# Second batch's mixing term moved from TensorE quarters to the ordinary path, with nine low parts on GpSimd

## The chip, the core and the metric

The kernel runs on one core of a Trainium2 chip. Its engines run side by side, each working through its own queue in order: TensorE (PE; its weight loads are shown as PEld), VectorE (DVE), ScalarE (ACT), GpSimd (POOL), and SyncE (SP), which only starts DMAs here. The metric is the device time of one launch in microseconds.

## What is computed

Sparse attention over 8 batches, 8 heads, 576 positions of 64 columns, and then a mixing and feed-forward layer:

```python
mask_local = (rel >= 0) & (rel < 32)                      # heads 0..3
mask_strided = (rel >= 0) & (key % 32 == query % 32)      # heads 4..7
x = softmax(q k^T / 8, masked) @ v                        # x: [8, 576, 512] over all heads
u = x + (x^T @ U @ V)^T                                   # U: [576, 32], V: [32, 576]
out = u + relu(u @ w_ch1) @ w_ch2                         # w_ch1: [512, 2048], w_ch2: [2048, 512]
```

`U`, `V` and the two weight matrices arrive as 64-bit floats, everything else as 32-bit. Both feed-forward products take each operand as a high part (rounded) and a low part (the rest): three passes of TensorE per product, high by high, high by low, low by high.

## The kernel before

**Feed-forward steps.** The 8 x 576 rows are worked off as nine blocks of 512 rows: block n < 8 has the first 512 rows of batch n, block 8 the last 64 of all batches. Each block runs 16 steps `fc`, one for every 128 hidden columns: `gemm1` (12 passes of 128 rows by 512 columns into `ph`), ScalarE's ReLU to the high part `gh`, VectorE's low part `gl`, and `gemm2` (12 passes into the accumulator `acc`). In program order `gemm1(fc + 1)` stands ahead of `gemm2(fc)`. A "slot" is half a step, so a block has 32 slots. I call the weights of one `fc` a weight block, w0 to w15.

**What runs between the steps.** While block n is multiplied, the next batch's attention is advanced by a generator (`advance`): a table (`A_EARLY` for block 0, `A_LATE` for the later ones) says from which slot to which it is spread and over how many pieces. For batches from 2 on (`NSP = 2`) the strided heads don't go to TensorE: in `strided_heads`, GpSimd multiplies (L440 for scores, L468 for the output; 27 pieces each, `tmp`) and VectorE sums each piece (L442, L470). `S0` and `S1` say in which slot that begins and ends. The strided heads' q, k and v come in the tile `st`.

**Start.** `first_attention` does batches 0 and 1 before the first feed-forward block and into it, all heads on TensorE. Batch 0 then goes straight into the transposed form that `gemm1` reads (`uh`, `ul`), by pairs of heads, in `quarter`: TensorE transposes x (L316), multiplies it by U (L282, L284) and adds V's product into the same bank (L293). For batch 1, `attention(1)` does the same four quarters during block 0's steps, and puts the sum into `raw`, which `split` turns into `uh` and `ul` when block 0 ends. For these two batches `gemm2` of step 0 also adds V's product to the accumulator (L667), since the untransposed x stays without it.

**Later batches.** `mix_t` multiplies x by U in two halves (L511, L515; VectorE adds the parts, L522, and makes the low part, L526), `mix_u` makes u in place (TensorE L534, VectorE L536), `mix_tail` does the last 64 rows (L543, L549), and `transposes` turns u with VectorE (L623) into `bt`, from which 32 DMAs fill `raw`.

**Weights.** Weight blocks 0 to 6 come as halves (`w0a`: the `gemm1` half, `w0b`: the `gemm2` half), 7 to 15 whole (128 x 1024). `weights` converts each in program order, some four steps ahead of its use: ScalarE takes the upper words (L124), VectorE makes three passes (L126, L127, L129), ScalarE casts the high part (L202) and VectorE subtracts it for the low part (L203). The buffers of `cv` are three, shared with `bt` and with later q, k, v loads. `load_ahead` starts the loads; GpSimd copies of one word (L166) hold each until its buffer may be overwritten.

**Who sets the order.** The framework schedules the instructions of each engine from the program's order and its own timing model; `tc.issue_after(i)` puts what it encloses behind instruction `i` on `i`'s own engine only.

Of the kernel before, what the change touches and what calls it, by code (L numbers as in the profile page):

```python
# [36 lines left out]
def fused_kernel(ctx, tc, pairs, strided, U, V, w_in, masks, eye, out):  # L37
# [147 lines left out]
    def weights():  # L185
        for i, (fc, x) in enumerate(units):
# [16 lines left out]
            nc.vector.tensor_tensor(out=parts[:, :, 1], in0=fv, in1=parts[:, :, 0].bitcast(F32), op=ALU.subtract)  # L203
# [65 lines left out]
    def quarter(b, pr):

        main, last_x, p0 = parts[b, pr]
        by_class = pr >= 2
# [7 lines left out]
        with tc.issue_after(lead):  # L280
            for t in range(4):
                nc.tensor.matmul(pm, Um[:, t, :], main[:, t, :], start=t == 0 and not (b and by_class), stop=False,  # L282
                                 skip_group_check=True, tile_position=(0, 0))
            nc.tensor.matmul(pm, Um[p0:p0 + 64, 4, :], last_x, start=False, stop=True, skip_group_check=True,  # L284
                             tile_position=(p0, 0))
# [11 lines left out]
        if b:  # L297
            dst = raw[:, :, :, pr, :]
            nc.scalar.copy(out=dst, in_=src.rearrange("p (s a) x -> p s a x", s=4) if by_class else
                           src.rearrange("p (s a x) -> p s a x", s=4, a=4))  # L300
        else:
            hi, lo = (u[:, pr, :].rearrange("p (j c) -> p j c", c=32) if by_class else u[:, pr, :] for u in (uh, ul))
            one = nc.scalar.copy(out=hi, in_=src)
            two = nc.vector.tensor_tensor(out=lo, in0=src, in1=hi.bitcast(F32), op=ALU.subtract)
            marks["split0"] = (two.ins, one.ins)
# [342 lines left out]
    def gemm1(fc, dcs=range(NDC)):  # L648
# [7 lines left out]
        nc.scalar.activation(out=gh, in_=ph, func=AF.Relu)  # L656
# [4 lines left out]
    def gemm2(n, fc, gh, gl):  # L661
        if fc == 0:
            accs[n] = [ps_acc.tile([128, 2, 512], F32, name="acc") for _ in range(2)]
        for s in range(4):
            cs = slice(128 * s, 128 * s + 128)
            if fc == 0 and n < NSP:
                nc.tensor.matmul(accs[n][s // 2][:, s % 2, :], Vst[:, cs], tsts[n], start=True, stop=False)  # L667
            for i, (gt, part) in enumerate(((gh, 0), (gh, 1), (gl, 0))):
                nc.tensor.matmul(accs[n][s // 2][:, s % 2, :], gt[:, cs], w_parts[fc, 1][:, part, :],  # L669
                                 start=(fc == 0 and i == 0 and n >= NSP), stop=(fc == NFC - 1 and i == 2))  # L670
# [159 lines left out]
```

## Time and profile before

| what | value |
|---|---|
| three runs | 940.04, 940.11, 940.59 us (median 940.11) |
| the profiled execution | 940.45 us, of it 938.7 us span |
| TensorE busy | 909.2 us, 97% of the span |
| VectorE, ScalarE, GpSimd busy | 561.6, 247.2, 325.7 us |
| TensorE's granted clock over the span | 0.993 |
| bytes moved | 74.24 MB |

Times in the profile are counted from the start of the span. A row of a timeline has the start, the length, the engine, the source line, the operation, output and input tile with shape, and in brackets how long the engine stood idle before it and what released it. A row of a group has the count, the busy time in us and the mean length in ns. Lengths of matmuls are modelled and overlap, so the spacing of the pieces in the chain of waits is what a pass costs there.

### The profile page before, as it was taken

How to read it: one execution, taken by the hardware profiler on the slowest of the kernel's cores; microseconds unless marked ns; L12 is line 12 of the kernel's file. 1: busy time of each engine (PE TensorE's matmuls, PEld its weight loads, DVE VectorE, ACT ScalarE, POOL GpSimd, SP SyncE). 2: the span in 40 equal slices, each digit the busy share in tenths (PEclk: the TensorE clock that was granted, in tenths of full speed). 3: DMA queues.
4: the chain of work that ended last, by engine and by line, in shares of the span. 5: the costliest groups of instructions: out<-in, count | busy, mean ns of one | idle time of the engine just before them, and what ended most of it. 6: DMA issues, size and time to landing. Idle time of an engine off the chain costs nothing.

```text
span 938.7 us, 16860 instructions
## 1 busy us (share of the span) xinstructions
PE 909.2 (97%) x7032; PEld 727.3 (77%) x7032; DVE 561.6 (60%) x907; ACT 247.2 (26%) x485; POOL 325.7 (35%) x374
## 2 busy tenths in 40 slices
PE   5789999999899999999999999999999999999997
PEld 4667888777677778777887788778877888888885
DVE  4679987757786678666776677657764341122111
ACT  4436542115122412151114221421233111121110
POOL 1213018434854385346644565447440000000000
PEclk9999999999989999999999999999999999999999
DMA  9958210200250114101420142013300231001001
GB/s 349 340 193 343 88 62 26 97 1 26 61 180 3 32 41 166 42 1 60 138 72 2 51 157 72 2 51 99 119 2 1 57 112 23 1 1 46 1 0 45
DMA packets 36780, 74.24 MB, mean 79 GB/s; under 512 B 5952, under 2 KB 20672, under 8 KB 34784
## 3 DMA queue, kind: packets, MB, share of 16 engines
q1 hardware_dynamic: 26464, 66.60, 20.1%
q10 hardware_dynamic: 9280, 4.20, 1.9%
q0 software_dynamic: 960, 2.36, 0.8%
q8 instruction: 55, 0.90, 0.4%
q14 instruction: 21, 0.17, 0.1%
HBM read 54.14 MB, written 11.67 MB: 70 GB/s over the span
## 4 chain that ended last, share of the span: by engine, by line
PE 83%; DVE 6%; POOL 5%; DMA 3%; issue 2%; ACT 1%; SPq 0%; DVEq 0%; POOLq 0%
PE acc L669 38%; PE ph L652 37%; POOL tmp L440 5%; DVE st L470 1%; PE px L380 1%; DMA w1a<-in_w_dram 1%; PE px L346 1%; PE px L367 1%; DMA w2a<-in_w_dram 1%; DMA late<-in_pairs_dram 1%; PE px L511 1%; DMA st<-in_strided_dram 1%; DVE gl L657 1%; PE px L534 1%; DVE s_st L442 0%
## 5 line engine op out<-in xcount | busy, mean ns | idle before, releaser
L657 DVE SCALAR_TENSOR_TENSOR gl<-ph,gh 128x512 fp32r<-128x512 f32 x144 | 98.8, 688 | 224.2 <-ACT gh L656 223.6
L652 PE MATMUL ph<-uh,w 128*128 128x512 f32 x648 | 215.0, 392 | 0.0
L656 ACT ACTIVATE gh<-ph 128x512 fp32r<-128x512 f32 x144 | 86.1, 598 | 471.2 <-PE ph L652 388.9
L440 POOL TENSOR_TENSOR tmp<-st 128x576 f32<-128x576 f32 (+6 forms) x162 | 168.7, 1082 | 114.0 <-DMA st<-in_strided_dram 58.3
L468 POOL TENSOR_TENSOR tmp<-st,s_st 128x448 f32<-128x448 f32 (+7 forms) x162 | 136.5, 873 | 183.7 <-DVE st L470 97.5
L669 PE MATMUL acc<-w,gh 128*128 128x512 f32 x648 | 197.6, 393 | 0.0
L470 DVE TENSOR_REDUCE st<-tmp 128x64 f32<-128x64 f32 (+8 forms) x162 | 137.6, 882 | 15.4 <-POOL tmp L468 14.3
L669 PEld LDWEIGHTS acc<-w,gh 128*128 128x128 f32 x648 | 122.2, 189 | 25.6
L652 PEld LDWEIGHTS ph<-uh,w 128*128 128x128 f32 x648 | 121.3, 188 | 26.4 <-issue 0.4
L652 PE MATMUL ph<-ul,w 128*128 128x512 f32 x324 | 126.8, 391 | 0.0
L669 PE MATMUL acc<-w,gl 128*128 128x512 f32 x324 | 122.2, 393 | 2.1 <-DVE gl L657 2.0
L442 DVE TENSOR_REDUCE s_st<-tmp 128x9 f32<-128x576 f32 (+6 forms) x162 | 87.6, 564 | 26.6 <-POOL tmp L440 25.7
L669 PEld LDWEIGHTS acc<-w,gl 128*128 128x128 f32 x324 | 61.4, 189 | 16.7 <-DVE gl L657 3.2
L652 PEld LDWEIGHTS ph<-ul,w 128*128 128x128 f32 x324 | 60.8, 188 | 12.9
L485 ACT COPY xg<-st 32x256 f32<-32x256 f32 x96 | 38.8, 404 | 8.5 <-DVE st L470 7.2
L522 DVE TENSOR_TENSOR ta<-px,ta 32x256 f32<-32x256 f32 x36 | 15.1, 420 | 33.1 <-ACT ta L520 32.3
L675 DVE TENSOR_TENSOR xg<-acc,xg 128x512 f32<-128x512 f32 x36 | 22.9, 681 | 9.3 <-PE acc L669 9.3
L644 DVE TENSOR_TENSOR ul<-raw,uh 128x512 fp32r<-128x512 f32 x32 | 24.7, 800 | 2.7 <-ACT uh L643 2.7
L652 PE MATMUL ph<-uh,w6a 128*128 128x512 f32 x72 | 25.1, 398 | 0.0
L652 PE MATMUL ph<-uh,w0a 128*128 128x512 f32 x72 | 24.8, 403 | 0.0
L652 PE MATMUL ph<-uh,w1a 128*128 128x512 f32 x72 | 24.1, 391 | 0.0
L652 PE MATMUL ph<-uh,w5a 128*128 128x512 f32 x72 | 23.8, 391 | 0.0
(292 smaller groups left out, 1272.4 us busy)
## 6 DMA issues: line engine op xcount, KB each, us to landing
w<-in_w_dram SPq DMA_DIRECT2D x9, 1024.0 KB, 8.6
out_dram<-xg SPq DMA_DIRECT2D x32, 256.0 KB, 2.1
v<-in_pairs_dram SPq DMA_DIRECT2D x12, 585.0 KB, 4.7
st<-in_strided_dram SPq DMA_DIRECT2D x6, 1152.0 KB, 5.6
qk<-in_pairs_dram SPq DMA_DIRECT2D x12, 576.0 KB, 5.1
late<-in_pairs_dram SPq DMA_DIRECT2D x8, 585.0 KB, 8.7
late<-in_pairs_dram SPq DMA_DIRECT2D x8, 576.0 KB, 9.7
raw<-bt SPq DMA_DIRECT2D x112, 32.0 KB, 1.9
```

The costliest lines, as they stand in the source:

```text
L440: nc.gpsimd.tensor_tensor(out=tmp[:, 0:n], in0=sk[:, j0:j0 + n], in1=sq[:, i:i + 1].broadcast_to([128, n, D]), op=ALU.mult)
L442: late.append(lambda tmp=tmp, n=n, i=i, j0=j0: nc.vector.tensor_reduce(out=s_st[:, i, j0:j0 + n], in_=tmp[:, 0:n], axis=AX.X, op=ALU.add))
L468: nc.gpsimd.tensor_tensor(out=tv, in0=sv[:, 0:i + 1, d0:d0 + step], in1=s_st[:, i, 0:i + 1].broadcast_to([128, i + 1, step]), op=ALU.mult)
L470: late.append(lambda tv=tv, i=i, d0=d0, step=step: nc.vector.tensor_reduce(out=o_st[:, i, d0:d0 + step], in_=tv.rearrange("p j d -> p d j" ...
L485: nc.scalar.copy(out=xg[32 * i4:32 * i4 + 32, :, cs], in_=o_st[rows, i4:16:4, :])
L522: nc.vector.tensor_tensor(out=ta, in0=ps_a[32 * j:32 * j + 32, :], in1=ta, op=ALU.add)
L644: nc.vector.tensor_tensor(out=lo, in0=raw[:, :, :, dc, :], in1=hi.bitcast(F32), op=ALU.subtract)
L652: nc.tensor.matmul(ph, w_parts[fc, 0][:, part, 128 * dc:128 * dc + 128], ut[:, dc, :], start=(dc == dcs[0] and i == 0), stop=(dc == dcs[-1 ...
L656: nc.scalar.activation(out=gh, in_=ph, func=AF.Relu)
L657: low = nc.vector.scalar_tensor_tensor(out=gl, in0=ph, scalar=0.0, in1=gh.bitcast(F32), op0=ALU.max, op1=ALU.subtract)
L669: nc.tensor.matmul(accs[n][s // 2][:, s % 2, :], gt[:, cs], w_parts[fc, 1][:, part, :], start=(fc == 0 and i == 0 and n >= NSP), stop=(fc ...
L675: nc.vector.tensor_tensor(out=ot, in0=accs[n][s // 2][:, s % 2, :], in1=ot, op=ALU.add)
```

## The change

For batch 1 the quarters are dropped: `attention(1)` now runs `mix_t`, `mix_u`, `mix_tail` and `transposes` as for later batches, the extra passes of `gemm2` stay for block 0 alone, and `A_EARLY` spreads 20 pieces over slots 2 to 28 (9 over 2 to 24 before). The low parts of weight blocks 7 to 15 are subtracted by GpSimd. A conversion's ScalarE pass is put behind a ScalarE instruction as well as its VectorE passes behind a VectorE one. The strided heads of batch 2 are due from slot 14 to slot 46 (20 to 52 before), and their load of `st` waits for a one-word GpSimd copy of weight block 9. In `first_attention` two loads swap places, and the second copy of U moves into spare columns of a `late` tile.

```diff
-N_EARLY = 9
+N_EARLY = 20
-A_EARLY = (2, 24, N_EARLY)
+A_EARLY = (2, 28, N_EARLY)
-S0 = {2: 20, **{b: 32 * (b - 1) - 12 for b in range(3, 8)}}
-S1 = (20, 14)
+S0 = {2: 14, **{b: 32 * (b - 1) - 12 for b in range(3, 8)}}
+S1 = (14, 14)
...
-        nc.scalar.copy(out=U_c.rearrange("p t r -> p (t r)"), in_=f[:, 5 * R:10 * R])
+        nc.scalar.copy(out=late[0][:, 1816:1816 + 5 * R], in_=f[:, 5 * R:10 * R])
...
             if i < N_HALF:
-                behind = marks["less"][min(7, i + 2)]
+                behind = marks["less"][min(7, i + 2)], marks["PT"][min(7, i + 1)]
             else:
-                behind = marks["gl"][fc - BEHIND]
-            with tc.issue_after(behind):
+                behind = marks["gl"][fc - BEHIND], marks["gh"][fc - BEHIND]
+            with tc.issue_after(behind[0]), tc.issue_after(behind[1]):
                 to_f32(raws[i], cv, 128, n)
...
-            nc.vector.tensor_tensor(out=parts[:, :, 1], in0=fv, in1=parts[:, :, 0].bitcast(F32), op=ALU.subtract)
+            (nc.vector if i < N_HALF else nc.gpsimd).tensor_tensor(out=parts[:, :, 1], in0=fv, in1=parts[:, :, 0].bitcast(F32),
+                                                                   op=ALU.subtract)
...
-        with tc.issue_after(marks["gl"][9]):
-            dma(out=st, in_=strided[b - NSP, :, 0:2 * NCH * D])
+        if b == NSP:
+            nc.gpsimd.tensor_copy(out=st[0:1, 0:1], in_=word_of[units.index((9, None))])
+        dma(out=st, in_=strided[b - NSP, :, 0:2 * NCH * D])
...
         for k, pair in enumerate(heads[0:4]):
             next(pair)
+            if k > 1:
+                load_ahead(k - 1)
             next(pair)
...
-            if k > 1:
-                load_ahead(k - 1)
...
         else:
-            tail = mix_tail(0)
-            next(tail)
-            yield
-            for pr in ORDER1:
-                quarter(b, pr)
-                yield
-            yield from tail
-            yield from mix_tail(1)
+            yield from mix_tail(0)
+            for half in range(2):
+                yield from mix_t(b, half)
+            yield from mix_u(b)
+            yield from mix_tail(b)
+            yield from transposes(b)
...
-            if fc == 0 and n < NSP:
+            if fc == 0 and n == 0:
                 nc.tensor.matmul(accs[n][s // 2][:, s % 2, :], Vst[:, cs], tsts[n], start=True, stop=False)
```

What the schedule makes of it is shown at three places, by the rows of an engine's queue in order. Lines of the changed kernel differ from those before by up to eight: its L202 is L203 before, its L125, L126, L128 are the conversion's L126, L127, L129, its L434 and L436 are L440 and L442, its L649 is the low part L657, its L530 is `mix_u`'s L536, and its L615 is the transposes' L623. Names like `w_1369` are whole weight blocks.

GpSimd in block 0, before, from the last of the one-word copies that hold the loads:

```order
L166 CAST w_1664<-w6b 1x1
L429 MEMSET s_st 128x324
L440 ISA
L440 TENSOR_TENSOR tmp<-st 128x64
L440 TENSOR_TENSOR tmp<-st 128x128
L440 TENSOR_TENSOR tmp<-st 128x192
```

The same place after:

```order
L165 CAST w_1697<-w6b 1x1
L202 ISA
L202 TENSOR_TENSOR w_1272<-cv,w_1272 128x2x512
L202 TENSOR_TENSOR w_1320<-cv,w_1320 128x2x512
L202 TENSOR_TENSOR w_1369<-cv,w_1369 128x2x512
L419 CAST st<-w_1369 1x1
L202 TENSOR_TENSOR w_1417<-cv,w_1417 128x2x512
L202 TENSOR_TENSOR w_1469<-cv,w_1469 128x2x512
L434 TENSOR_TENSOR tmp<-st 128x64
L434 TENSOR_TENSOR tmp<-st 128x128
```

Five subtractions (weight blocks 7 to 11) now stand ahead of the first score multiply, and the other four stand among the multiplies, after the 4th, 10th, 15th and 21st of the 27.

VectorE before, from the low part `gl` of step 8 to that of step 9:

```order
L657 SCALAR_TENSOR_TENSOR gl<-ph,gh 128x512
L126 TENSOR_SCALAR cv<-cv 128x1024
L203 TENSOR_TENSOR w_1528<-cv,w_1528 128x2x512
L127 SCALAR_TENSOR_TENSOR cv<-w_1560,cv 128x1024
L129 SCALAR_TENSOR_TENSOR cv<-w_1560,cv 128x1024
L291 TENSOR_TENSOR tst<-px,tst 32x128
L203 TENSOR_TENSOR w_1568<-cv,w_1568 128x2x512
L657 SCALAR_TENSOR_TENSOR gl<-ph,gh 128x512
```

VectorE after, from the low part of step 8 to that of step 9:

```order
L649 SCALAR_TENSOR_TENSOR gl<-ph,gh 128x512
L126 SCALAR_TENSOR_TENSOR cv<-w_1517,cv 128x1024
L125 TENSOR_SCALAR cv<-cv 128x1024
L128 SCALAR_TENSOR_TENSOR cv<-w_1517,cv 128x1024
L126 SCALAR_TENSOR_TENSOR cv<-w_1574,cv 128x1024
L530 TENSOR_TENSOR xg<-px,xg 128x512 x2
L615 STREAM_TRANSPOSE bt<-xg 128x4x4x32 x2
L436 TENSOR_REDUCE s_st<-tmp 128x1
L436 TENSOR_REDUCE s_st<-tmp 128x2
L649 SCALAR_TENSOR_TENSOR gl<-ph,gh 128x512
```

The subtractions are gone from this queue; `mix_u`, the transposes and the first sums of the strided scores have come in between the conversion passes (before, the first such sum stood behind the low part of step 10).

SyncE in the prefix, before:

```order
L95 DMA w1a<-in_w_dram 128x512
L95 DMA st<-in_strided_dram 128x2304
L95 DMA late<-in_pairs_dram 128x1152 x2
L95 DMA late<-in_pairs_dram 128x1170
L95 DMA late<-in_pairs_dram 128x1152
L95 DMA w2a<-in_w_dram 128x512
```

SyncE after, at the end of the weight loads:

```order
L95 DMA w_1697<-in_w_dram 128x1024
L95 DMA st<-in_strided_dram 128x2304
L95 DMA raw<-bt 32x2x128 x5
L95 DMA ud<-xt 128x512
L95 DMA raw<-bt 32x2x128 x11
```

The load of `st` has moved from between `w1a` and the q, k, v tiles of the second batch to behind the last weight load, and 16 of the second batch's 32 `raw` loads follow it (the other 16 are started by ScalarE).

More of the change, by code (lines that the diff above doesn't have):

```diff
@@ L260, in early_pair @@
             far_dma(out=od[512:576, oc:oc + 2 * D], in_=last_x)
-        parts[b, pr] = (main, last_x, p0)
+        if b == 0:
+            parts[pr] = (main, last_x, p0)
         if last:
@@ L265, in early_pair, with quarter @@
         if b == 0:
-            quarter(b, pr)
+            quarter(pr)
             yield
-    def quarter(b, pr):
-        main, last_x, p0 = parts[b, pr]
+    def quarter(pr):
+        main, last_x, p0 = parts[pr]
         by_class = pr >= 2
         cs = slice(2 * pr * D, 2 * pr * D + 2 * D)
-        Um = U_c if by_class else U_sb
+        Um = late[0][:, 1816:1816 + 5 * R].rearrange("p (t r) -> p t r", r=R) if by_class else U_sb
         pu = psx2().rearrange("p a x -> p (a x)")
-        pm = ps_h.tile([128, 512], F32, name="ph")[0:32, 0:128] if b == 0 else pu[0:32, 640:768]
+        pm = ps_h.tile([128, 512], F32, name="ph")[0:32, 0:128]
         lead = x_transposed(pu, [main[:, t, :] for t in range(4)])
@@ L281, in quarter @@
             for t in range(4):
-                nc.tensor.matmul(pm, Um[:, t, :], main[:, t, :], start=t == 0 and not (b and by_class), stop=False,
+                nc.tensor.matmul(pm, Um[:, t, :], main[:, t, :], start=t == 0, stop=False,
                                  skip_group_check=True, tile_position=(0, 0))
@@ L285, in quarter @@
                              tile_position=(p0, 0))
-        if b not in tsts:
-            tsts[b] = ap_.tile([96, DM], F32R, name="tst", **({"tag": "att", "bufs": ATT_BUFS} if b else {}))
-        tst = tsts[b]
+        tst = tsts[0]
         nc.scalar.copy(out=tst[0:32, cs], in_=pm)
@@ L296, in quarter @@
             src = pu[:, 0:S].rearrange("p (c j) -> p j c", j=NCH)[:, 0:16, :]
[L297 to L305, printed above, removed]
+        hi, lo = (u[:, pr, :].rearrange("p (j c) -> p j c", c=32) if by_class else u[:, pr, :] for u in (uh, ul))
+        nc.scalar.copy(out=hi, in_=src)
+        nc.vector.tensor_tensor(out=lo, in0=src, in1=hi.bitcast(F32), op=ALU.subtract)
     parts = {}
@@ L655, in gemm1 @@
         gl = mp.tile([128, 512], F32R, name="gl", bufs=2)
-        nc.scalar.activation(out=gh, in_=ph, func=AF.Relu)
+        marks.setdefault("gh", []).append(nc.scalar.activation(out=gh, in_=ph, func=AF.Relu).ins)
         low = nc.vector.scalar_tensor_tensor(out=gl, in0=ph, scalar=0.0, in1=gh.bitcast(F32), op0=ALU.max, op1=ALU.subtract)
@@ L669, in gemm2 @@
                 nc.tensor.matmul(accs[n][s // 2][:, s % 2, :], gt[:, cs], w_parts[fc, 1][:, part, :],
-                                 start=(fc == 0 and i == 0 and n >= NSP), stop=(fc == NFC - 1 and i == 2))
+                                 start=(fc == 0 and i == 0 and n > 0), stop=(fc == NFC - 1 and i == 2))
     def finish(n):
```

6 lines of the change are left out of this document (2 added, 4 removed).

## The prediction

> **What bounds the kernel now.** I began with the page's busy shares and its chain of waits.
>
> ```profile
> PE 909.2 (97%) x7032; PEld 727.3 (77%) x7032; DVE 561.6 (60%) x907; ACT 247.2 (26%) x485; POOL 325.7 (35%) x374
> PE 83%; DVE 6%; POOL 5%; DMA 3%; issue 2%; ACT 1%; SPq 0%; DVEq 0%; POOLq 0%
> ```
>
> TensorE is nearly full, so a pass taken from it is worth its time wherever it isn't waiting. Where it waits I looked for in the timeline of TensorE and in windows: the third weight block's first pass in blocks 1, 2 and 3, the two longest late waits, the clock around them, and then three stretches of the start.
>
> ```profile
> 182.59 0.39 PE L652 MATMUL ph<-uh,w3a 128*128 128x512 f32 x1
> 287.55 0.39 PE L652 MATMUL ph<-uh,w3a 128*128 128x512 f32 x1
> 384.86 0.39 PE L652 MATMUL ph<-uh,w3a 128*128 128x512 f32 x1
> 255.93 0.43 PE L340 MATMUL px<-masks_sb 128*128 128x320 bf16 x2 [2.43 <-DVE xt L549]
> 259.81 0.79 PE L669 MATMUL acc<-w,gl 128*128 128x512 f32 x1 [1.98 <-DVE gl L657]
> 250.00:260.00 10.00, 5.59 (x23) 3.80 (x22) 8.79 (x16) 1.10 (x2) 10.00 (x10) 0.83 0.41 95
> 260.00:270.00 10.00, 9.89 (x36) 7.65 (x37) 7.54 (x14) 3.12 (x7) 4.83 (x4) 0.83 0.42 144
> ...
> 0.00:50.00 50.00, 34.01 (x859) 25.13 (x859) 26.53 (x50) 21.03 (x41) 8.32 (x20) 1.00 0.95 341
> 50.00:101.20 51.20, 49.14 (x675) 37.98 (x676) 47.01 (x82) 27.01 (x43) 11.89 (x27) 0.97 0.72 269
> 101.20:154.20 53.00, 53.00 (x250) 43.55 (x249) 43.02 (x57) 22.28 (x31) 16.30 (x16) 1.00 0.12 39
> ```
>
> (A window's columns: length; busy us of TensorE, its loads, VectorE, ScalarE, GpSimd; clock; DMA share; GB/s.) From block 1 to block 2 it is 104.96 us, from 2 to 3 only 97.31: block 1 loses 7.65. Two waits of 2.43 and 1.98 us and a clock of 0.83 over 20 us (3.4 us) make 7.8, so they are the loss. Up to 50 us the DMAs are full (0.95); up to 101.2, the low part of step 5, VectorE is (47.01 of 51.2); to 154.2, the low part of step 14, TensorE is, with VectorE at 43.02.
>
> **TensorE's quarters.** One quarter of a local pair in the chain, then half a `mix_t`, then one L667:
>
> ```profile
> 108.25 0.89 PE px L316 x8
> 109.14 0.99 PE px L282 x8
> 110.14 0.33 PE px L284 x2
> 116.81 0.23 PE px L293
> 214.13 0.57 PE px L511 x8
> 214.69 0.29 PE px L515 x8
> 173.64 0.23 PE acc L667
> ```
>
> Out go four quarters at 2.44 (9.76; the strided pairs' fifth transpose is left out) and four L667 in block 1 (0.92). In come two halves of `mix_t` at 0.86 (1.72) and four `mix_u` products of L667's size (0.92); `mix_tail` stays. That is 8.0 us less. The trace says that it lies on the path after 101.2. Ahead of that VectorE sets the pace, and there its queue gets shorter too, so I count all of it: by the order, two L126, two L127, one L129 and one L203 of whole blocks no longer stand ahead of step 5's low part, 6.3 us, against three L522 and an L526 (0.69 like an L126) that come in, 1.9.
>
> ```profile
> L126 DVE TENSOR_SCALAR cv<-cv 128x1024 int32<-128x1024 int32 x9 | 6.2, 684 | 0.0
> L127 DVE SCALAR_TENSOR_TENSOR cv<-w,cv 128x1024 int32<-128x1024 int32 x9 | 11.2, 1248 | 0.1
> L129 DVE SCALAR_TENSOR_TENSOR cv<-w,cv 128x1024 int32<-128x1024 int32 x9 | 11.0, 1220 | 0.4
> L203 DVE TENSOR_TENSOR w<-cv,w 128x1024 fp32r<-128x1024 f32 x9 | 11.0, 1223 | 1.6 <-ACT w L202 1.6
> L522 DVE TENSOR_TENSOR ta<-px,ta 32x256 f32<-32x256 f32 x36 | 15.1, 420 | 33.1 <-ACT ta L520 32.3
> ```
>
> **Block 1's stall.** Batch 2's strided output was summed late, and 13 score sums of batch 3 stood in VectorE's queue in one step, ahead of L549 and of the low part. After the change the output sums end at step 8 of block 1 instead of step 10, and from step 9 on VectorE's queue has the rows of block 2, step by step. So I take the whole 7.65; the bounds are 0 and 7.65.
>
> **The prefix.** `st` no longer loads among the first tiles.
>
> ```profile
> 23.66 8.33 DMA w2a<-in_w_dram
> ...
> st<-in_strided_dram SPq DMA_DIRECT2D x6, 1152.0 KB, 5.6
> ...
> 137.90 23.84 POOL L440 TENSOR_TENSOR tmp<-st 128x192 f32<-128x192 f32 x22 [41.53 <-DVE xt L549]
> ```
>
> 1152 KB at 341 GB/s are 3.5 us of a full DMA stretch, behind which `w2a` waits 8.33 us on the chain. The gain lies between 0 and 3.5; I take 2, since TensorE stands idle 16 of these 50 us and not all of that is for DMAs. The held conversion passes only reorder ScalarE and VectorE here, at nothing, with that idle time as cover. The load's new place costs nothing as long as it lands before GpSimd is free: now GpSimd waits 41.53 us, to 137.90, for a buffer that `mix_tail` of batch 1 held; after, `st` is started behind the subtraction of block 9 and is there 5.6 us later, some 25 us earlier than that. What is queued behind its one-word copy (the subtractions of 10 and 11) doesn't need `st`. The 32 `raw` starts, half of them on ScalarE between `gh`s, are covered by a ScalarE that is busy 22.28 of 53 us; without that cover `gh`, then TensorE, would come late.
>
> **What it costs: VectorE against GpSimd.** The nine subtractions and the multiplies now run beside the conversion; before, the multiplies began when it ended. Prices on GpSimd, then two places where both engines met, an undisturbed L644 for comparison, and when a low part is written and first read:
>
> ```profile
> L440 POOL TENSOR_TENSOR tmp<-st 128x576 f32<-128x576 f32 (+6 forms) x162 | 168.7, 1082 | 114.0 <-DMA st<-in_strided_dram 58.3
> ...
> L440 POOL TENSOR_TENSOR tmp<-st 128x576 f32<-128x576 f32 x66 | 94.2, 1436 | 3.3 <-DVE s_st L442 3.3
> L440 POOL TENSOR_TENSOR tmp<-st 128x64 f32<-128x64 f32 x12 | 4.5, 376 | 58.4 <-DMA st<-in_strided_dram 58.3
> L468 POOL TENSOR_TENSOR tmp<-st,s_st 128x576 f32<-128x576 f32 x18 | 20.6, 1161 | 24.1 <-DVE st L470 24.1
> L468 POOL TENSOR_TENSOR tmp<-st,s_st 128x64 f32<-128x64 f32 x6 | 1.8, 294 | 47.9 <-DVE s_st L459 47.9
> ...
> 158.35 3.94 DVE L644 TENSOR_TENSOR ul<-raw,uh 128x512 fp32r<-128x512 f32 x1
> 157.80 3.94 POOL L440 TENSOR_TENSOR tmp<-st 128x576 f32<-128x576 f32 x3
> 164.68 1.40 DVE L644 TENSOR_TENSOR ul<-raw,uh 128x512 fp32r<-128x512 f32 x1
> 164.24 1.30 POOL L440 TENSOR_TENSOR tmp<-st 128x512 f32<-128x512 f32 x1 [2.50 <-DVE s_st L442]
> 162.21 0.68 DVE L644 TENSOR_TENSOR ul<-raw,uh 128x512 fp32r<-128x512 f32 x1
> ...
> 154.23 0.69 DVE L657 SCALAR_TENSOR_TENSOR gl<-ph,gh 128x512 fp32r<-128x512 f32 x1 [0.53 <-ACT gh L656]
> 159.30 0.39 PE L669 MATMUL acc<-w,gl 128*128 128x512 f32 x1
> ```
>
> A VectorE pass with two operands in SBUF takes 0.68 alone, 3.94 when it starts inside three back-to-back multiplies and 1.40 inside one: it ends 0.55 after the GpSimd instruction does. So it waits for GpSimd, and GpSimd for it. L127, L129 and the subtraction have two such operands. L126 has one; I count it with them because it stands between them in the queue (without it the sum below is 5.5 lower).
>
> The subtraction itself isn't in the trace at this size: extended along L468's two rows 128x1024 is 1.92 us, along L440's 2.36; I take 2.1, the middle, having no reason for either. Between the low parts of steps 5 and 14 stand eight subtractions (16.8), 21 multiplies at 1.082 (22.7) and, on VectorE, L126, L127, L129 of eight weight blocks (8 x 3.15 = 25.2): 64.7 us if one side goes at a time. TensorE needs for this stretch 53.0, less two quarters and the last product of a third (5.1), plus half a `mix_t` and the `mix_u` (1.8): 49.7. The excess is 15; 4.4 of it are free, because a low part is written by 154.92 and read at 159.30, as now. So some 10 us of new waiting. Below it is bounded by 0 (39.5 on GpSimd and under 43 on VectorE would both fit beside 49.7), above by about 20, where VectorE also loses an extra multiply of 1.08 at every second of the 24 passes and the conversion's three buffers come free late.
>
> The Trainium skill, page "SBUF — State Buffer", section "SBUF: two separate sides", says that VectorE and GpSimd share a port pair that one of them takes exclusively for a whole instruction, VectorE whenever it has two SBUF inputs. By that rule the 64.7 us are serial and the sum is the one below; without it the subtractions are free and it ends near 922. The rows of L644 agree with it.
>
> **The sum**, against the profiled execution's 940.45: -8.0 -7.65 -2 +10 = 932.8; the median of the runs is 0.3 lower, so 932.5.
>
> **Rivals.**
> - *The cover holds.* GpSimd is busy only 16.30 of the 53 us now, and sums and low parts don't collide; then the 10 us are 0 and it is 922.5. Against it: the two L644.
> - *VectorE starves, and it gets slower.* The place is block 0 from step 6 on. The first L644 lost to two further multiplies that started after it, so passes may wait for whole runs of GpSimd instructions; low parts queue behind them, TensorE waits, and the clock falls as it did behind the 2.43 us wait. From a cost of 17.7 us (8.0 + 7.65 + 2) on, the change loses. At 20, with 2 more for the clock, it is 944.5. For it: 22 multiplies in a row at 137.90 leave few gaps. Against it: GpSimd stops after a few pieces, when the buffers of `tmp` wait for VectorE's sums.
> - *Block 1's stall stays*, because block 0's lateness is handed on to the strided chain: 932.5 + 7.65 = 940.2, no change. Against it: the order equal to block 2's.
>
> **Chances.** The forecast (927 to 938) 0.5, the cover holds 0.2, slower 0.2, the stall stays 0.1. A measurement tells about 0.2% (1.9 us) from no change: 938.2 to 942.0. Faster has the first two and a third of the last, 0.73; no change most of the rest of the last, 0.07; slower 0.20. From 922 to 942.5 all but 0.2 is held.
>
> **What would show it.** Right: L316 and L293 on `px` gone, and from block 1 to block 2 about 97.3 us; `w2a` landing about 3 us earlier; L127 and L129 beside GpSimd longer than their 1.25 us, subtractions near or over 2.1, TensorE waiting in block 0 for `gl`, some 10 us between steps 5 and 14. Wrong: no such waits (then 922), or waits of more than 2 us in most steps, a low clock in block 0, `ph` waiting for a late low part of blocks 12 to 15 (then 940 and over), or a period of 105 us still.

## The result, and the profile after

The changed kernel takes 934.34 us (median of four runs, 933.03 to 936.00); the kernel before took 940.29 (four runs, 940.04 to 940.59). The ratio is 0.9933, with an interval of [0.9921, 0.9946]: faster, by 6 us. The forecast was 932.5, from 922 to 942.5. The profiled execution took 934.02 us, of it 932.2 span.

The page of the changed kernel, busy shares and the chain by engine:

```profile
PE 899.3 (96%) x6982; PEld 716.6 (77%) x6982; DVE 568.2 (61%) x910; ACT 243.6 (26%) x478; POOL 360.0 (39%) x384
PE 85%; DVE 5%; POOL 4%; issue 3%; DMA 1%; ACT 0%; SPq 0%; DVEq 0%; ACTq 0%; POOLq 0%
```

TensorE is busy for 9.9 us less, GpSimd for 34 more. VectorE, which gave away nine subtractions, is busier than before (568.2 against 561.6). Where the time went is told by the third weight block's first pass in blocks 0 to 3, in TensorE's timeline:

```profile
67.17 0.40 PE L644 MATMUL ph<-uh,w3a 128*128 128x512 f32 x1
...
182.64 0.39 PE L644 MATMUL ph<-uh,w3a 128*128 128x512 f32 x1
...
280.95 0.39 PE L644 MATMUL ph<-uh,w3a 128*128 128x512 f32 x1
...
378.26 0.39 PE L644 MATMUL ph<-uh,w3a 128*128 128x512 f32 x1
```

I call the time from one such pass to the next "block 0" and "block 1". The windows between them, of the kernel before:

```profile
69.80:182.59 112.79, 111.38 (x660) 89.65 (x659) 97.85 (x146) 47.90 (x72) 39.11 (x50) 1.00 0.35 128
182.59:287.55 104.96, 100.44 (x741) 78.93 (x739) 73.29 (x120) 25.43 (x55) 56.00 (x62) 0.97 0.19 61
```

and of the changed kernel (length; busy TensorE, its loads, VectorE, ScalarE, GpSimd; clock; DMA share; GB/s):

```profile
67.17:182.64 115.47, 106.29 (x605) 81.63 (x604) 106.58 (x153) 43.45 (x64) 76.97 (x63) 0.97 0.42 144
182.64:280.95 98.31, 98.31 (x745) 78.19 (x744) 71.22 (x118) 26.81 (x57) 52.47 (x58) 1.00 0.20 65
```

Block 1 is 6.65 us shorter and TensorE has no idle time in it. Block 0 is 2.68 us longer although TensorE's work in it fell: it was idle for 1.41 us of it before and is for 9.18 now, and the clock went from 1.00 to 0.97. TensorE's four longest waits there, in its timeline:

```profile
76.62 0.64 PE L505 MATMUL px<-xg,U_sb 128*32 128x256 f32 x8 [1.68 <-ACT cv L123]
...
118.50 0.50 PE L661 MATMUL acc<-w,gl 128*128 128x512 f32 x1 [1.49 <-DVE gl L649]
...
126.30 0.54 PE L537 MATMUL px<-tst,Vst 96*128 96x512 f32 x1 [2.07 <-DVE xg L530]
...
128.40 0.80 PE L661 MATMUL acc<-w,gl 128*128 128x512 f32 x1 [1.57 <-DVE gl L649]
```

and VectorE's first entry in the list of waits of block 0 (us in total, times, longest):

```profile
DVE s_st L436 <- POOL tmp L434: 7.3, 8, 2.6
```

The last three of TensorE's are for VectorE; the first, at `mix_t`, is for ScalarE with a conversion pass. With 106.58 us busy and 7.3 waiting for multiplies, VectorE fills 113.9 of the 115.47. The conversion's groups of the changed kernel (nine weight blocks each; busy, mean ns) say with what:

```profile
L202 POOL TENSOR_TENSOR w<-cv,w 128x1024 fp32r<-128x1024 f32 x9 | 26.9, 2990 | 9.4 <-ACT w L201 4.4 <-issue 2.8 <-DMA st<-in_strided_dram 2.3
L128 DVE SCALAR_TENSOR_TENSOR cv<-w,cv 128x1024 int32<-128x1024 int32 x9 | 15.7, 1745 | 0.1
L126 DVE SCALAR_TENSOR_TENSOR cv<-w,cv 128x1024 int32<-128x1024 int32 x9 | 12.3, 1363 | 0.0
L125 DVE TENSOR_SCALAR cv<-cv 128x1024 int32<-128x1024 int32 x9 | 10.7, 1188 | 0.0
```

The 27 passes took 6.2 + 11.2 + 11.0 = 28.4 us before and take 38.7 now. So VectorE was rid of 11.0 us of subtractions and got 10.3 back in longer passes. How one grows is seen in the timelines of GpSimd (the first subtraction and the last) and of VectorE at the first:

```profile
95.73 4.04 POOL L202 TENSOR_TENSOR w<-cv,w 128x1024 fp32r<-128x1024 f32 x1 [0.36 <-ACT w L201]
...
156.64 2.38 POOL L202 TENSOR_TENSOR w<-cv,w 128x1024 fp32r<-128x1024 f32 x1
...
95.70 0.67 DVE L202 TENSOR_TENSOR w6b<-cv,w6b 128x512 fp32r<-128x512 f32 x1
96.30 1.21 DVE L126 SCALAR_TENSOR_TENSOR cv<-w,cv 128x1024 int32<-128x1024 int32 x1
97.54 0.42 DVE L516 TENSOR_TENSOR ta<-px,ta 32x256 f32<-32x256 f32 x1
97.88 2.43 DVE L125 TENSOR_SCALAR cv<-cv 128x1024 int32<-128x1024 int32 x1
100.24 1.21 DVE L128 SCALAR_TENSOR_TENSOR cv<-w,cv 128x1024 int32<-128x1024 int32 x1
```

The first subtraction starts 0.03 us after a low part of VectorE's and gets behind L126 too; those run at their own pace (0.67, 1.21), and it takes 4.04 us instead of the 2.38 of the last. Then L125, otherwise 0.68, takes 2.43 and ends 0.54 after the subtraction does. L516, which reads PSUM and one tile in SBUF, is not slowed at all. Passes that grew in this way stand ahead of TensorE's three waits for VectorE, in VectorE's timeline:

```profile
109.69 2.83 DVE L128 SCALAR_TENSOR_TENSOR cv<-w,cv 128x1024 int32<-128x1024 int32 x1
...
119.50 2.88 DVE L125 TENSOR_SCALAR cv<-cv 128x1024 int32<-128x1024 int32 x1
```

The first sum that waits for a multiply comes only at 131.31 us, for 0.18. So the longer passes are enough for these three waits, without the 7.3 us that sums wait.

### The profile page after: what moved, and what is told of

Its sections match the earlier page's. It is cut to its first block, busy times and chain, and to the rows that moved or that the text cites. A ratio compares the mean times of both kernels' runs of the same rounds, so it can differ in the third digit from the quotient of the medians.

```text
span 932.2 us, 16818 instructions
## 1 busy us (share of the span) xinstructions
PE 899.3 (96%) x6982; PEld 716.6 (77%) x6982; DVE 568.2 (61%) x910; ACT 243.6 (26%) x478; POOL 360.0 (39%) x384
## 3 DMA queue, kind: packets, MB, share of 16 engines
q0 software_dynamic: 960, 2.36, 0.9%
## 4 chain that ended last, share of the span: by engine, by line
PE 85%; DVE 5%; POOL 4%; issue 3%; DMA 1%; ACT 0%; SPq 0%; DVEq 0%; ACTq 0%; POOLq 0%
PE acc L661 39%; PE ph L644 38%; POOL tmp L434 3%; PE px L339 1%; DVE cv L128 1%; DMA late<-in_pairs_dram 1%; PE px L373 1%; POOL w L202 1%; DVE cv L126 1%; PE px L360 1%; PE px L505 1%; PE acc L373 1%; PE px L528 1%; PE px L333 0%; DVE ul L636 0%
## 5 line engine op out<-in xcount | busy, mean ns | idle before, releaser
L649 DVE SCALAR_TENSOR_TENSOR gl<-ph,gh 128x512 fp32r<-128x512 f32 x144 | 98.8, 687 | 217.9 <-ACT gh L648 217.3
L644 PE MATMUL ph<-uh,w 128*128 128x512 f32 x648 | 215.0, 392 | 0.7 <-POOL w L202 0.7
L434 POOL TENSOR_TENSOR tmp<-st 128x576 f32<-128x576 f32 (+6 forms) x162 | 175.4, 1121 | 73.6 <-DMA st<-in_strided_dram 49.1
L464 DVE TENSOR_REDUCE st<-tmp 128x64 f32<-128x64 f32 (+8 forms) x162 | 137.1, 880 | 13.4 <-POOL tmp L462 12.4
L644 PEld LDWEIGHTS ph<-uh,w 128*128 128x128 f32 x648 | 121.6, 188 | 27.2 <-POOL w L202 1.1
L644 PE MATMUL ph<-ul,w 128*128 128x512 f32 x324 | 127.2, 393 | 0.0
L436 DVE TENSOR_REDUCE s_st<-tmp 128x9 f32<-128x576 f32 (+6 forms) x162 | 87.3, 562 | 21.7 <-POOL tmp L434 21.0
L644 PEld LDWEIGHTS ph<-ul,w 128*128 128x128 f32 x324 | 61.1, 189 | 13.1
L516 DVE TENSOR_TENSOR ta<-px,ta 32x256 f32<-32x256 f32 x42 | 17.6, 420 | 36.3 <-ACT ta L514 35.3
L202 POOL TENSOR_TENSOR w<-cv,w 128x1024 fp32r<-128x1024 f32 x9 | 26.9, 2990 | 9.4 <-ACT w L201 4.4
L530 DVE TENSOR_TENSOR xg<-px,xg 128x512 f32<-128x512 f32 x28 | 18.0, 684 | 13.1 <-PE px L528 13.1
L644 PE MATMUL ph<-uh,w6a 128*128 128x512 f32 x72 | 25.1, 398 | 0.0
L644 PE MATMUL ph<-uh,w0a 128*128 128x512 f32 x72 | 24.2, 395 | 0.0
```

The costliest lines, as they stand in the source:

```text
L202: (nc.vector if i < N_HALF else nc.gpsimd).tensor_tensor(out=parts[:, :, 1], in0=fv, in1=parts[:, :, 0].bitcast(F32), op=ALU.subtract)
L434: nc.gpsimd.tensor_tensor(out=tmp[:, 0:n], in0=sk[:, j0:j0 + n], in1=sq[:, i:i + 1].broadcast_to([128, n, D]), op=ALU.mult)
L436: late.append(lambda tmp=tmp, n=n, i=i, j0=j0: nc.vector.tensor_reduce(out=s_st[:, i, j0:j0 + n], in_=tmp[:, 0:n], axis=AX.X, op=ALU.add))
L464: late.append(lambda tv=tv, i=i, d0=d0, step=step: nc.vector.tensor_reduce(out=o_st[:, i, d0:d0 + step], in_=tv.rearrange("p j d -> p d j" ...
L644: nc.tensor.matmul(ph, w_parts[fc, 0][:, part, 128 * dc:128 * dc + 128], ut[:, dc, :], start=(dc == dcs[0] and i == 0), stop=(dc == dcs[-1 ...
L649: low = nc.vector.scalar_tensor_tensor(out=gl, in0=ph, scalar=0.0, in1=gh.bitcast(F32), op0=ALU.max, op1=ALU.subtract)
```

## The experiments

Each ratio is to runs of the kernel before on the same chip, between those of the experiment (their medians lay between 939.7 and 940.4 us). Blocks 0 and 1 come from the profiled execution.

| kernel | median us | ratio, interval | block 0 | block 1 |
|---|---|---|---|---|
| before | 940.29 | | 112.79 | 104.96 |
| the change | 934.34 | 0.9933 [0.9921, 0.9946] | 115.47 | 98.31 |
| before_strided_from_14 | 934.60 | 0.9946 [0.9930, 0.9963] | 114.18 | 98.11 |
| subs_on_vector | 936.95 | 0.9970 [0.9958, 0.9982] | 118.30 | 97.36 |
| strided_from_20 | 944.15 | 1.0042 [1.0025, 1.0059] | 115.71 | 106.70 |
| st_load_early | 951.15 | 1.0122 [1.0101, 1.0143] | 128.57 | 98.13 |
| passes_not_held | 937.64 | 0.9973 [0.9962, 0.9984] | 117.11 | 98.23 |
| no_score_multiplies | 933.79 | 0.9941 [0.9925, 0.9958] | 117.12 | 97.34 |
| low_parts_left_out | 922.73 | 0.9806 [0.9784, 0.9829] | 105.48 | 97.49 |
| shift_left_out | 932.63 | 0.9909 [0.9887, 0.9930] | 114.03 | 98.23 |
| strided_from_20_behind_13 | 936.16 | 0.9956 [0.9940, 0.9973] | 111.07 | 104.25 |
| strided_from_24_behind_15 | 944.81 | 1.0054 [1.0042, 1.0067] | 111.78 | 113.21 |
| strided_batch3_from_64 | 943.16 | 1.0022 [1.0009, 1.0035] | 111.10 | 99.08 |
| vector_subs_strided_from_20 | 931.42 | 0.9916 [0.9890, 0.9941] | 111.96 | 98.64 |

### Where the 6 us come from: one part alone, and that part undone

before_strided_from_14, against the kernel before:

```diff
-S0 = {2: 20, ...}          S1 = (20, 14)
+S0 = {2: 14, ...}          S1 = (14, 14)
-        with tc.issue_after(marks["gl"][9]):
+        with tc.issue_after(marks["gl"][6]):
```

> The kernel before with one part alone: batch 2's strided heads due from slot 14 to slot 46 (the load of st stays where it was). The theory: the stall of block 1 goes with this alone; from block 1 to block 2 97 to 99 us (104.96 now), the rest at most 3 us worse by multiplies beside the conversion: 932 to 936.5. The rival: quarters and subtractions on VectorE keep block 0 late, the chain is not earlier for being asked earlier, and it stays at 940 or goes above.

strided_from_20, against the changed kernel:

```diff
-S0 = {2: 14, ...}          S1 = (14, 14)
+S0 = {2: 20, ...}          S1 = (20, 14)
```

> The changed kernel with batch 2's strided heads due from slot 20 to slot 52 again. The theory: the earlier start is what took the 6.65 us out of block 1, and it is what brings the multiplies into block 0 beside the conversion. So from block 1 to block 2 it is about 105 us again (98.31 now), and steps 5 to 14 of block 0 take some 3 to 6 us less than 63.1: 935 to 938 in all. The rival: block 1's stall went because batch 1's quarters left block 0 and the conversion ended earlier; then the period stays near 98 and the time is 928 to 931.

The windows of blocks 0 and 1, of before_strided_from_14:

```profile
67.49:181.67 114.18, 112.46 (x660) 89.83 (x659) 106.39 (x157) 47.66 (x72) 51.14 (x61) 1.00 0.36 126
181.67:279.78 98.11, 98.11 (x740) 77.78 (x739) 64.80 (x109) 25.39 (x55) 47.30 (x51) 1.00 0.20 65
```

and of strided_from_20:

```profile
69.63:185.34 115.71, 107.23 (x610) 82.43 (x609) 103.50 (x147) 44.87 (x66) 71.50 (x56) 0.97 0.43 143
185.34:292.04 106.70, 101.64 (x740) 79.94 (x739) 74.32 (x121) 25.29 (x55) 56.62 (x63) 0.95 0.18 60
```

The two numbers that ask for batch 2's strided heads six slots earlier take block 1 from 104.96 to 98.11 by themselves, and the median to 934.60, which can't be told from the whole change. (The third line moves a hold; the load of `st` is issued at 11.3 us there and at 12.0 before.) Taken out of the changed kernel, the stall is back (106.70) and the kernel is slower than before. So that is the gain: beside it the rest of the change sums to about nothing, and without it the rest costs some 4 us (1.0042). The order behind it: the first score sum of batch 3 comes 54.7 us into block 1 before, 56.2 in strided_from_20, 47.2 in the change and 46.4 in before_strided_from_14. My second expectation of strided_from_20 failed: block 0 didn't get shorter (115.71), since the multiplies begin behind the fifth subtraction all the same, at 123.69 us against 121.78 in the change; 944.15 instead of 935 to 938.

### What eats TensorE's saving in block 0

Two theories stand against each other. In the one, the "lock", VectorE's conversion passes and GpSimd's instructions go one at a time; in the other VectorE is full of its own work. shift_left_out and low_parts_left_out take away, in turn, work of VectorE's own and GpSimd's subtractions:

```diff
-        nc.vector.tensor_scalar(out=i, in0=i, scalar1=3, ...)
+        if n < 1024:
+            nc.vector.tensor_scalar(out=i, in0=i, scalar1=3, ...)
```

> The changed kernel without VectorE's shift pass L125 for weight blocks 7 to 15 (so these weights have wrong values; 9 passes of 1.19 us, 10.7 us of VectorE's own work, gone; GpSimd's work as it is). If VectorE's own work fills block 0: block 0 shortens by 6 to 10 us to 105 to 109, and the time is 925 to 929. If it is the lock with GpSimd that paces it (L126 and L128, which need GpSimd to stand still, are all still there, and GpSimd's 77 us): block 0 shortens by 0 to 3 us, and the time is 931 to 935.

```diff
-            (nc.vector if i < N_HALF else nc.gpsimd).tensor_tensor(out=parts[:, :, 1], ... op=ALU.subtract)
+            if i < N_HALF:
+                nc.vector.tensor_tensor(out=parts[:, :, 1], ... op=ALU.subtract)
+            else:
+                nc.scalar.copy(out=parts[:, :, 1], in_=fv)
```

> The changed kernel without the nine subtractions of weight blocks 7 to 15 on any engine (ScalarE copies the converted weights into the low part's place, so the low parts are wrong; 9 x 1.2 us more on ScalarE, which is busy 43 of 115 us). It shows what the subtractions cost where they stand, on GpSimd. If they cost by the lock: the 27 conversion passes of 128x1024 fall from 38.7 us to 29 to 31, the multiplies come to GpSimd earlier and VectorE's 7.3 us of waiting for them go; block 0 takes 106 to 109 us where it took 115.5, and the time is 925 to 929. If VectorE's own passes fill block 0, whatever GpSimd does: batch 2's sums move up into the room and block 0 stays at 112 us or more; 931 to 935.

Block 0 of shift_left_out:

```profile
66.60:180.63 114.03, 105.06 (x606) 81.28 (x604) 103.67 (x148) 43.82 (x65) 74.43 (x65) 0.99 0.43 146
```

and the conversion's groups there (its L129 and L127 are L128 and L126 of the changed kernel):

```profile
L129 DVE SCALAR_TENSOR_TENSOR cv<-w,cv 128x1024 int32<-128x1024 int32 x9 | 17.5, 1942 | 0.0
L127 DVE SCALAR_TENSOR_TENSOR cv<-w,cv 128x1024 int32<-128x1024 int32 x9 | 16.4, 1827 | 0.7 <-ACT cv L123 0.7
```

Block 0 of low_parts_left_out:

```profile
68.81:174.29 105.48, 103.81 (x611) 82.02 (x609) 100.06 (x160) 52.41 (x74) 56.04 (x60) 0.98 0.47 158
```

and the groups:

```profile
L128 DVE SCALAR_TENSOR_TENSOR cv<-w,cv 128x1024 int32<-128x1024 int32 x9 | 12.5, 1389 | 0.0
L126 DVE SCALAR_TENSOR_TENSOR cv<-w,cv 128x1024 int32<-128x1024 int32 x9 | 11.8, 1315 | 0.0
L125 DVE TENSOR_SCALAR cv<-cv 128x1024 int32<-128x1024 int32 x9 | 6.3, 703 | 0.9 <-ACT cv L123 0.8
```

Without the shift VectorE has 10.7 us less to do and block 0 gains 1.44: L126 and L128 grow from 28.0 to 33.9 us. Without the subtractions VectorE's own passes are all there and block 0 gains 9.99; TensorE is idle for 1.67 us of it, all of it the wait for ScalarE at `mix_t`. Both blocks speak for the lock and against the rival: 1.44 where 0 to 3 was its number, 105.48 where it had 106 to 109; the time of low_parts_left_out, 922.73, is below its 925 to 929. The two effects of the subtractions are not parted here: with them go most of the longer passes and most of the sums' waiting for products (3.0 us instead of 7.3).

no_score_multiplies asks whether the multiplies do as much:

```diff
+                if b > NSP:
                     nc.gpsimd.tensor_tensor(out=tmp[:, 0:n], in0=sk[...], in1=sq[...], op=ALU.mult)
-                late.append(lambda tmp=tmp, ...
+                late.append(lambda tmp=tmp if b > NSP else sk[:, j0:j0 + n], ...
```

> The changed kernel without GpSimd's 27 score multiplies of batch 2 (the products are left out: VectorE sums the same number of elements straight from st, so its own work stays). The theory of the lock: the conversion passes are stretched by multiplies and subtractions (38.7 us for the 27 passes of 128x1024, 28.4 undisturbed), and VectorE's sums wait in its queue for multiplies (7.3 us in block 0). Without the multiplies only the subtractions collide: the passes take 31 to 34 us, the 7.3 us are gone, block 0 (the first to the second third-block pass) takes 107 to 109 us where it took 115.5, and the time falls by 5 to 8 us to 926 to 929. The rival, that VectorE is full in block 0 by its own passes since mix_t, mix_u and transposes of batch 1 came in (9 us): nothing of VectorE's work has gone, block 0 stays at 113 us or more, the time at 932 to 935.

Block 0 of no_score_multiplies:

```profile
69.10:186.22 117.12, 106.76 (x610) 82.38 (x609) 107.62 (x161) 44.63 (x66) 46.38 (x43) 0.97 0.41 142
```

and the longest wait of TensorE in it, in its timeline:

```profile
130.61 0.80 PE L538 MATMUL px<-tst,Vst 96*128 96x512 f32 x1 [4.43 <-DVE xg L531]
```

A miss: GpSimd's work in block 0 fell from 76.97 to 46.38 us, and block 0 isn't shorter; 117.12 and 933.79 are what the rival had. The passes fell only from 38.7 to 35.7 us. The kernel is no clean test between the two, because the sums, no longer waiting for products, moved up in VectorE's queue: 15 of them stand between the low parts of steps 8 and 9, and TensorE waits 4.43 us for an L531 there. What the multiplies alone cost is better read from low_parts_left_out, which has all of them: 30.6 us for the 27 passes and no wait of TensorE for VectorE. So it is the subtractions that bring the cost. What the multiplies add beside them no run here shows by itself.

subs_on_vector puts the subtractions back:

```diff
-            (nc.vector if i < N_HALF else nc.gpsimd).tensor_tensor(out=parts[:, :, 1], ...
+            nc.vector.tensor_tensor(out=parts[:, :, 1], ...
```

> The changed kernel with one part undone: VectorE subtracts all low parts again (nine L202 back from GpSimd). The theory: in block 0, passes of VectorE with two operands in SBUF and GpSimd's instructions go one at a time, and GpSimd's subtraction (2.99 us in its place) costs that sum more than VectorE's (1.22 us). Between the low parts of steps 5 and 14 the sum falls from 16.8 + 22.7 + 25.2 = 64.7 us to 22.7 + 8 x (3.15 + 1.22) = 57.7, so the stretch falls from 63.1 us to about 57 and the time from 934.3 to about 928; L125, L126 and L128 come back towards 0.7, 1.25 and 1.22 us. The rival: VectorE is simply full there (50.07 of 53 us) and the subtractions relieve it; then 9 x 1.22 = 11 us come on top of it, the stretch grows to 70 us or more, and the time is 940 to 945.

Block 0 of subs_on_vector:

```profile
70.80:189.10 118.30, 107.24 (x610) 83.05 (x609) 114.58 (x167) 45.79 (x66) 56.96 (x53) 0.96 0.40 136
```

and the two longest waits of TensorE in it:

```profile
139.71 0.73 PE L644 MATMUL ph<-uh,w 128*128 128x512 f32 x2 [2.58 <-DVE w L202]
...
154.59 0.80 PE L661 MATMUL acc<-w,gl 128*128 128x512 f32 x1 [5.26 <-DVE gl L649]
```

Another miss: 118.30 instead of a shorter block 0, 936.95 instead of 928. The serial sum would have it shorter; the rival's 940 to 945 didn't come either. TensorE is idle for 11.06 us in this block, 7.84 of them in these two places, where a crowd of score sums and conversion passes stands ahead of one low part. Whether that is VectorE being full or this order was open, and the last experiment was for that.

### Where batch 2's strided heads stand

```diff
-S0 = {2: 14, ...}    word_of[units.index((9, None))]
+S0 = {2: 20, ...}    word_of[units.index((13, None))]    # strided_from_20_behind_13
+S0 = {2: 24, ...}    word_of[units.index((15, None))]    # strided_from_24_behind_15
+S0 = {2: 20, 3: 64, ...}  ...(13, None)                  # strided_batch3_from_64
```

> The changed kernel with batch 2's strided heads due from slot 20 to slot 46 (14 to 46 now) and st held by the word of weight block 13 (9 now), so that GpSimd has eight subtractions ahead of the first multiply and one between the multiplies. The theory of the lock: the multiplies leave steps 7 to 12, so that the stretch from step 5 to step 14 falls from 63.1 us to 53 to 57; the chain is still asked to end at slot 46, so block 1 keeps 98 to 100 us: 927 to 931 in all. The rival: the sums that leave block 0 stand in VectorE's queue in block 1, which grows by as much (104 us or more): 934 to 938.

> As the kernel behind block 13, but from slot 24 and behind weight block 15: no multiply stands ahead of a subtraction. The theory of the lock: the subtractions meet only the conversion passes, the stretch from step 5 to step 14 is 51 to 55 us, the low parts on GpSimd take 2.4 to 2.8 us each; block 1 has the 27 multiplies and their sums in its first steps and loses 2 to 5 us of that: 927 to 933. The rival (VectorE is full in block 0 anyway): the stretch stays over 58 us and block 1 grows to 104 us: 938 to 942.

> A version meant to beat both: as the kernel with batch 2's strided heads from slot 20 and st behind weight block 13 (block 0 111.1, block 1 104.3 us), and batch 3's strided heads from slot 64 (52 before). There, block 1's stall was mix_tail's sum L543 of batch 2 behind ten score sums of batch 3 in one step; now three stand ahead of it. The theory: block 0 keeps 111 us and block 1 falls to 97.3 to 99, and batch 3's chain, late in block 2, costs that block 0 to 5 us: 927 to 932. The rival: the same stall comes in block 2 (104 us there): 934 to 937, no better than the change.

Blocks 0 and 1 of strided_from_20_behind_13, then blocks 1 and 2 of strided_batch3_from_64:

```profile
69.65:180.72 111.07, 105.09 (x605) 81.44 (x604) 102.18 (x142) 43.30 (x64) 61.85 (x47) 0.98 0.43 145
180.72:284.97 104.25, 101.25 (x746) 80.20 (x744) 75.24 (x125) 26.78 (x57) 58.62 (x67) 0.97 0.19 61
```

```profile
181.92:281.00 99.08, 98.31 (x746) 78.33 (x744) 61.62 (x100) 26.45 (x56) 41.69 (x48) 1.00 0.18 58
281.00:389.10 108.10, 102.31 (x741) 79.38 (x739) 82.10 (x138) 25.86 (x56) 68.34 (x75) 0.97 0.20 67
```

With the multiplies behind the subtractions block 0 falls by 4.4 us, and block 1 takes back 5.9; from slot 24 it takes back 14.9. With batch 3's heads later as well, block 1 is well (99.08) and block 2 has the stall (108.10). The theories had the direction of block 0 (its stretch from step 5 to step 14 took 57.5 and 58.6 us with batch 2's chain later, 63.1 in the change), and the rivals had the whole, two of them still too low: the work that leaves block 0 comes again as a stall in the next block, where ten score sums of the following batch then stand ahead of `mix_tail`'s sum L543.

### The hold of the passes and the gate of `st`

```diff
-            with tc.issue_after(behind[0]), tc.issue_after(behind[1]):
+            with tc.issue_after(behind[0]):                         # passes_not_held
-        if b == NSP:
-            nc.gpsimd.tensor_copy(out=st[0:1, 0:1], in_=word_of[...])  # st_load_early
```

> The changed kernel with a conversion's ScalarE pass no longer held behind a ScalarE instruction (only behind the VectorE one, as before the change). The prediction's theory: the hold only reorders and costs nothing, so the time stays within 2 us of 934.3. The rival: without it the ScalarE pass of a conversion stands ahead of gh or of the attention's exponentials, TensorE waits for those, and it is 3 to 6 us longer.

> The changed kernel without the one-word copy that holds the load of st, so that its 1152 KB go back among the first tiles. The theory of the prediction: the prefix loses its gain; the first pass of the third weight block comes at 69 to 70 us (67.17 now), and the whole is 2 to 2.6 us longer, 936.3 to 937. The rival: block 0 is paced by VectorE and GpSimd, whose work does not start earlier for an earlier TensorE, and so it takes the delay up: 934 to 935.

TensorE's longest wait in block 0 of passes_not_held:

```profile
126.25 0.70 PE L661 MATMUL acc<-w,gl 128*128 128x512 f32 x1 [3.09 <-DVE gl L649]
```

Block 0 of st_load_early, the group of the last pass, and the first entry of TensorE's waits in block 0 (its L642 is L644):

```profile
71.00:199.57 128.57, 111.28 (x610) 84.63 (x609) 119.43 (x162) 45.78 (x66) 85.52 (x69) 0.95 0.36 120
```

```profile
L128 DVE SCALAR_TENSOR_TENSOR cv<-w,cv 128x1024 int32<-128x1024 int32 x9 | 19.4, 2160 | 0.0
```

```profile
PE ph L642 <- POOL w L202: 7.3, 4, 3.7
```

Without the hold it is 3 to 4 us longer than the change (ratios 0.9973 and 0.9933, intervals apart), outside my 2. TensorE doesn't wait for `gh`, as the rival had it, but for one low part (3.09 us) and, at `mix_t`, 2.96 us for VectorE's L385; block 0 has 1.64 of the 2.37 us by which its profiled execution is longer than the change's. Without the gate it is 951: neither theory had that. GpSimd, which has `st` early, takes multiplies ahead of and between the subtractions, the passes grow further (L128 to 2.16 us), and TensorE waits 7.3 us for weights that GpSimd hasn't finished. The one-word copy is worth 17 us here. 13.1 of them lie in block 0 and so in GpSimd's queue; 3.8 lie ahead of it: the third weight block's first pass comes at 71.00 us, hardly later than the 70.80 of subs_on_vector, which loads `st` late.

### A version against both

```diff
-            (nc.vector if i < N_HALF else nc.gpsimd).tensor_tensor(out=parts[:, :, 1], ...
+            nc.vector.tensor_tensor(out=parts[:, :, 1], ...
-S0 = {2: 14, ...}    word_of[units.index((9, None))]
+S0 = {2: 20, ...}    word_of[units.index((13, None))]
```

> A version meant to beat both: the changed kernel with all low parts on VectorE, batch 2's strided heads from slot 20 to slot 46, and st behind the word of weight block 13. With the low parts on VectorE from slot 14, block 0 took 118.3 us, of it a wait of 5.26 and one of 2.58 where ten score sums and the low part of a weight block stood ahead of one low part gl, and block 1 97.36. The theory of the lock: GpSimd has nothing but multiplies now, and they come after most conversion passes; block 0 takes 109 to 114 us and block 1 97.3 to 99, 927 to 932 in all. The rival: VectorE, with 11 us of subtractions more, is the bound whatever GpSimd does; block 0 stays at 117 us or more, 935 to 938.

Block 0 of vector_subs_strided_from_20:

```profile
67.45:179.41 111.96, 105.33 (x605) 81.40 (x604) 104.24 (x159) 44.99 (x65) 45.07 (x52) 0.98 0.43 149
```

and the conversion's groups:

```profile
L202 DVE TENSOR_TENSOR w<-cv,w 128x1024 fp32r<-128x1024 f32 x9 | 11.9, 1334 | 0.0
L126 DVE SCALAR_TENSOR_TENSOR cv<-w,cv 128x1024 int32<-128x1024 int32 x9 | 11.7, 1305 | 0.1
L128 DVE SCALAR_TENSOR_TENSOR cv<-w,cv 128x1024 int32<-128x1024 int32 x9 | 11.0, 1223 | 0.2
L125 DVE TENSOR_SCALAR cv<-cv 128x1024 int32<-128x1024 int32 x9 | 6.0, 679 | 0.0
```

VectorE now does passes and subtractions in 40.6 us together; in the changed kernel the passes alone took 38.7. Block 0 is 111.96 with the subtractions on VectorE, block 1 98.64 and the time 931.42, as the theory had them, so VectorE isn't simply full: subs_on_vector was long by its order. strided_from_20_behind_13 differs from this kernel in the place of the nine subtractions alone. On GpSimd they make block 0 hardly shorter (111.07) and block 1 5.61 us longer; the ratios are 0.9956 and 0.9916, with intervals that touch. With the strided heads from slot 14 it is the other way: 0.9933 with the subtractions on GpSimd, 0.9970 on VectorE, intervals apart. So which engine should subtract hangs on the order beside it. At 931.42 us vector_subs_strided_from_20 is the fastest kernel here that computes everything, but its interval [0.9890, 0.9941] and the change's overlap; that it beats the change is likely and not shown.

## Why the prediction was right

The sum was -8.0 -7.65 -2 +10. Its sign and its main mechanisms held. One term earned nothing that can be seen, the working of another was partly wrong, and that the total came within 2 us is in part luck.

- *TensorE's quarters, -8.0.* Confirmed: in low_parts_left_out, where nothing covers it, TensorE's work in block 0 is 103.81 us against 111.38, 7.57 less (at a clock of 0.98 against 1.00).
- *Block 1's stall, -7.65.* 6.65 in the change and 6.85 by the earlier start alone: 98.31 remains, not quite the 97.31 of later blocks. The reason given, an output that is summed earlier, is what the two strided experiments show.
- *The prefix, -2.* This term fell. The third weight block's first pass came 2.63 us earlier in the change, at 67.17, but in strided_from_20, whose loads and one-word copies up to there stand in the same order, at 69.63. The executions differ by as much as the gain. before_strided_from_14, with the early load of `st`, came there at 67.49. In part it goes with the granted clock: over the first 66 us it was 1.00 in the change, 0.97 before, 0.97 in before_strided_from_14 and 0.90 in strided_from_20. `w2a` does land 2.7 us earlier (29.3 against 32.0), which was the sign asked for, but it doesn't show in that pass. So the moved load earns nothing that can be seen, and leaving it out of the sum gives 934.5 for the median. That this is so near the measured 934.34 is luck, since effects of several us (the next two points) were in no term.
- *VectorE against GpSimd, +10.* 9.99, by low_parts_left_out. The size is right by luck, for the parts of it aren't. The term was waiting alone; measured are 7.51 us more idle time of TensorE (9.18 against 1.67) and 2.48 us in which its work took longer (106.29 against 103.81). From step 5 to step 14, where the 10 us were put, the low parts lie 63.14 us apart, 13.4 above the 49.7 of the prediction and 7.9 above low_parts_left_out (55.28). I had the subtraction at 2.1 us; it takes 2.99 on average and 2.38 with nothing in its way, which L440's rows extended (2.36) had said. I had the multiplies in the sum with 22.7 us; beside the conversion alone they make no wait. I hadn't seen that VectorE's queue would wait for products (7.3 us) which stand on GpSimd behind subtractions. L125, which I counted with some doubt, does wait.
- *The held passes at nothing.* Wrong by 3 to 4 us in the change's favour, without a term of its own in the sum. Nor was there one for the 1.68 us that `mix_t` now waits for ScalarE.
- *The rivals.* The cover doesn't hold: 922.5 was the price of that, and 922.73 came only with the subtractions left out. VectorE doesn't starve: the loss stayed nearly 8 us short of the 17.7 from which the change would have lost, though st_load_early shows how near that is. The stall of block 1 went, as the order of VectorE's queue had it.

The Trainium skill, page "Perfetto Trace Analysis", section "Optimizing Scalar/DVE Operations", warns that moving operations between VectorE and GpSimd might not help, since they share an SBUF port. The runs agree, with a number: 11.0 us moved away, 10.3 come back; of the two orders tried, one was faster for the move and one wasn't.

## What to carry to other kernels

Work that is moved from one engine to another has to be charged twice: with its time on the new engine, and with what it adds to every instruction of the old one that shares a resource with it; here the second was as large as what was moved. When a change has several parts, test the smallest alone: two numbers in a table were worth as much as the whole. A saving on the fullest engine is worth its time only where the next engine's queue can follow; look there for the next wait before counting it.

## What the hardware showed that I had not expected

- A VectorE pass with one operand in SBUF is held up by GpSimd as well: L125 took 0.68 us alone, 1.19 on average beside the subtractions, and 2.43 behind one. The low part `gl`, which reads PSUM and one tile in SBUF, kept its 0.69 us throughout. The Trainium skill, page "SBUF — State Buffer", section "SBUF: two separate sides", names VectorE's two-port mode besides two SBUF inputs as taking the shared pair; L125 agrees if its 0.68 us for 1024 elements, against 1.22 for L128, are that mode, which the trace doesn't say.
- Waits of 1.49 to 2.07 us were followed by a lower clock. In the change's block 0 these windows, behind the three waits for VectorE, have 0.83, and those before and after them 1.00:

```profile
120.00:130.00 10.00, 6.37 (x24) 4.68 (x23) 10.00 (x12) 2.20 (x2) 10.00 (x8) 0.83 0.04 10
130.00:140.00 10.00, 10.00 (x39) 7.90 (x38) 9.73 (x14) 3.12 (x4) 10.00 (x6) 0.83 0.24 69
```

  0.17 of 20 us is 3.4 us, an estimate of what that cost beside the waits. How much idle time a block has doesn't set its clock: shift_left_out has 8.97 us in block 0 at 0.99, low_parts_left_out 1.67 at 0.98.
- One and the same start reached the same pass at 67.17 and at 69.63 us in two executions, at a granted clock of 1.00 and 0.90 over the first 66 us; why the clock differed no run here shows. A difference of 2 us in the start can't be read from one profile of each kernel.
